# A transformer block on one core: the exact-table GELU of nine chunks becomes a tanh formula with its steps on GpSimd, and background matmuls may run as four column tiles

## The chip, the cores and the metric

The kernel runs on one core of a Trainium2 chip. A core has five engines, each with its own queue of instructions that it takes in order: TensorE (PE, matmuls; weight loads are listed apart as PEld), VectorE (DVE), ScalarE (ACT), GpSimd (POOL) and SyncE (SP, which here issues the DMAs). They meet through semaphores. The metric is the device time of one execution in microseconds; the time before is the median of three runs. In the profile a line number such as L1023 is a line of the kernel's file. Many operations are recorded through one helper and share its line (L426 in the kernel before, L435 in the changed one); those are told apart by the tiles that they write and read.

## The reference

```python
def _A_ref(x, wqkv, wo):                       # B, S, D = 1, 2048, 640; H = 32 heads of 20
    qkv = (x @ wqkv).reshape(B, S, 3, H, Dh) ...
    scores = jnp.einsum("bhqd,bhkd->bhqk", q, k) * (Dh ** -0.5)
    p = _softmax(scores, axis=-1)
    o = jnp.einsum("bhqk,bhkd->bhqd", p, v)
    return o ... @ wo

def _B_ref(x, w_gate, w_up, w_down):           # Df = 1728
    g = jnp.einsum("bsd,df->bsf", x, w_gate)
    u = jnp.einsum("bsd,df->bsf", x, w_up)
    h = _gelu(g) * u                           # jax.nn.gelu(approximate=True)
    return jnp.einsum("bsf,fd->bsd", h, w_down)

x = A_x
h = x + _A_ref(_layernorm(x), A_wqkv, A_wo)
h2 = h + _B_ref(_layernorm(h), B_w_gate, B_w_up, B_w_down)
```

All inputs and the output are bf16.

## The kernel before

**A planner sets every order.** The code does not issue instructions as it runs. It records operations (`Sched.op`) with an engine, an assumed length, a priority, the keys they read and write, and the PSUM banks they take and release. `Sched.schedule` then plays them through a model in Python and fixes each engine's order; `Sched.emit` writes that order out with the semaphore waits that the keys ask for. An engine on the chip keeps this order, so an instruction whose input is late holds back all that stands behind it on its engine. The planner knows the engines' lengths and semaphore delays; it has no notion of two engines that share a path to on-chip memory.

**Attention.** Scores are made as tiles of 128 keys x 512 (head and query pairs laid side by side): 2048 tiles, four heads to a *quad* of tiles. PE's score matmuls (L1023) use row tiles of 32 rows, up to four at once. A *unit* is three or two tiles in PSUM banks 0 to 2 or 3 and 4. ACT takes the exponential of a unit in one instruction of 1536 or 1024 columns and writes `pts` or `pts2` (in `rege`). The value matmuls (L426, out of `pts`, `rege` or others and `v_all`) use column tiles of 32 columns, four at once, and add up in bank 6. ACT can't do all exponentials in the time wanted, so some quads (78 of 512, by slot in `D_QUADS`; `D_LEAD` and `D_QUADS` also set when they start) are made on VectorE with integer tricks: each of their four tiles is evicted from PSUM by L967, then the quad takes three passes of 2048 columns that read and write SBUF alone (`d_exp`: a mask, a product, a mask). Their spare buffers are pieces of regions that are free at that time, such as old query blocks of `qt_all`.

**The MLP in the background.** The queries are cut into ten chunks (six of 256 rows, four of 128). While the attention of later chunks runs, `post` works on the chunk before: output projection, residual, layernorm (`ln_rsqrt`, whose dozen tiny steps run on POOL, and a normalise on DVE), a DMA transpose, then for blocks of up to 512 gate columns: gate matmuls (`mms`, L1227), GELU, up matmuls, product, and `down` (L1345). These matmuls use the whole array (mode `full`). PE pays some time when neighbouring matmuls change the tiling (modes `row`, `col`, `full`), and the planner charges `MODE_SWITCH` for it. `chain` makes the other background matmuls (L716: projections of queries, keys and values, and `wo`).

**GELU before.** In chunks 0 to 6 VectorE copies the gate block from PSUM, ACT applies its GELU table to up to 2048 columns at once, and VectorE multiplies by the up block. The GELU table is not the exponential's, so ACT loads a table ahead of it and another behind it; `MERGE = (0, 2, 5)` puts two chunks into one such block. In chunks 7 and 8 (`TANH`) GELU is worked out with the tanh, which needs no other table than the exponential's: three DVE steps (square, multiply-add, product) in `qt_all`, the tanh on ACT, then on DVE a step with the up block and a last product. The last chunk (`tail`) uses the GELU table after the last exponential, and is the same in both kernels.

**Zero matmuls.** Where the planner finds PE too little used over 3.4 us it adds column-tiled matmuls of zeros into bank 6 (`self.pad`, four of 512 columns a set) or a warm matmul, so that PE's clock stays up. `PAD_MIN` and `WARM_MIN` are the shares of use below which it does.

Of the kernel before, what the change touches and what calls it, by code (L numbers as in the profile page):

```python
# [7 lines left out]
ALU = mybir.AluOpType  # L8
AX = mybir.AxisListType
FP32 = mybir.dt.float32  # L10
BF16 = mybir.dt.bfloat16
# [7 lines left out]
WARM_WIN, WARM_MIN = 3.4, 0.53  # L19
PAD_WIN, PAD_MIN = 3.4, 0.46  # L20
QK_LEAD = 0.55
PE_AGE = 0.5
# [20 lines left out]
class Op:  # L43
    __slots__ = ("i", "eng", "fns", "dur", "lat", "prio", "deps", "succ", "nd", "ready",
                 "acq", "rel", "sem", "tag", "mode", "start", "fin", "pos", "know", "util")


class Sched:
# [15 lines left out]
    def op(self, eng, fns, dur, prio, reads=(), writes=(), acq=(), rel=(), after=(), sem=None, lat=None, mode=None, util=0.0):  # L64
# [6 lines left out]
        o.mode = mode  # L71
        o.tag = writes[0] if writes else None
# [24 lines left out]
    def schedule(self):  # L97
# [20 lines left out]
        live = begun = False  # L118
        due = None
        total = len(ops)  # L120
        while done < total:
# [6 lines left out]
            for e in ENGINES:  # L128
# [9 lines left out]
                while ready[e]:  # L138
# [8 lines left out]
                    if e == "pe" and due is not None and o.prio[0] > 0 and t < due < t + o.dur + (MODE_SWITCH[e] if mode[e] not in (None, o.mode) else 0):  # L147
                        skipped.append((p, i))
                        if len(skipped) >= 60:
                            break  # L150
                        continue
                    for bk in o.acq:
                        for b in bk.allowed:
                            if owner[b] is None and free_at[b] <= t + 1e-9 and b not in got and b not in kept:
                                got.append(b)
                                break
# [10 lines left out]
                    if chosen is None:  # L167
                        chosen, banks = o, got
                        if e != "pe" or p[0] < 1 or o.mode == mode[e] or t - o.ready > PE_AGE:
                            break  # L170
# [15 lines left out]
                if chosen is None:  # L186
                    if e == "pe" and self.warm is not None:
# [5 lines left out]
                        if sum(x for _, x in recent) < WARM_MIN * WARM_WIN and (free7 or live or free6):  # L193
# [3 lines left out]
                            o.acq, o.rel, o.succ, o.dur = [], [], [], 0.215  # L197
# [15 lines left out]
                t0 = t  # L213
                if o.i in self.heads:
                    self.spare = self.spares[o.tag[1]]
                    js, nk = self.heads[o.i]
# [144 lines left out]
FOUR = (28, 29)  # L361
PERM_C = 2
# [13 lines left out]
MERGE = (0, 2, 5)  # L376
TANH = (7, 8)
# [9 lines left out]
D_Q2 = 26  # L387
D_LAG = 2
D_QUADS = (0, 2, 3, 2, 2, 3, 2, 2, 3, 3, 3, 3, 3, 3, 2, 3, 2, 3, 4, 3, 2, 3, 3, 3, 2, 2, 2, 2, 2, 2, 2, 2, 0)
D_FIRST, D_PART = 2, 0.8  # L390
D_LEAD = ((0, 0, 0, 0, 0, 0, 0, 0), (0, 10, 12, 12, 12, 12, 12, 12, 12, 12, 12, 16, 16, 8, 8, 8, 12, 12, 12, 12, 12, 12, 12, 12, 8))
# [13 lines left out]
def bass_sequential_preLN__mha_block__glu_gated_geglu__prompt_kernel(  # L405
# [12 lines left out]
    with ExitStack() as es:  # L418
# [55 lines left out]
        def carver(reg, size):  # L474
            off = [0]

            def carve(n):
# [40 lines left out]
                 **{"q%d" % k: [qr[k][:, 0:2048], qr[k][:, 2048:4096]] for k in range(3)}}  # L518
# [193 lines left out]

        def chain(bk, key, n, steps, reads, prio, acq=True, after=()):
            cold = 0.1 if prio == P_PRO and not any(("xnT", tt) in reads for tt in range(4, NT)) else 0.0
            for k, (l, r) in enumerate(steps):
                yield op("pe", lambda eng, l=l, r=r, k=k: eng.matmul(  # L716
                    bank(bk, n), l, r, start=(k == 0), stop=(k == len(steps) - 1)),
                    c_mm(n) + cold, prio, mode="full", util=n / 2400.0, reads=reads, writes=[key], acq=[bk] if (k == 0 and acq) else [],
                    after=after if k == 0 else ())
# [204 lines left out]
        t_last = {}  # L924
# [6 lines left out]

        def q_free(k, lo, hi):
            return sum((tuple(last_qk[c]) for c, (q0, nq) in enumerate(QR) if c and q0 // 512 == k and lo <= q0 % 512 < hi), ())
# [4 lines left out]
        def d_regions(tile, u):  # L938
# [4 lines left out]
            return ("i",) * (tile[0] == 7) + ("k", "x", "w") + ("q0",) * (us >= 8) + ("q1",) * (us >= 16) + ("q2",) * (us >= D_Q2)  # L943

        def d_free(region):
# [4 lines left out]
            return q_done(int(region[1])) + tuple(t_last.get(4, ()) if region == "q2" else ())  # L950
# [11 lines left out]
        def d_exp(b, tile, prio, u, aft):  # L962
# [11 lines left out]
            d(I("tensor_tensor", y.bitcast(BF16), v.bitcast(BF16), y.bitcast(BF16), ALU.mult), 1.06, vk + yk, yk)  # L974
# [177 lines left out]
        gated, tanhs = [], []  # L1152
        t_last.clear()

        def post(c, first_banks, banks, tail):
# [50 lines left out]
            for tt in range(tb, tb + nt):  # L1206
# [5 lines left out]
                else:  # L1212
                    dma_transposes(o_nat[:, tt, :], [("on", g, tt) for g in range(NG)], hnT[:, :, tt * 128:(tt + 1) * 128], ("hnT", tt),
                                   after=first)
            p = P_LATE if c == len(CHUNKS) - 2 else P_BG
# [5 lines left out]
            def mms(k, w, wkey, after):  # L1221
                bk, key = Bank(*banks), ("bk", sc_id())
                for fi in range(min(fn_, NF - k * fn_)):
                    f = k * fn_ + fi
                    for a in range(NA):
# [3 lines left out]
                            start=(a == 0), stop=(a == NA - 1)),  # L1229
                           c_mm(nq), p, mode="full", util=nq / 2400.0, reads=hk + [(wkey, a)], writes=[key], acq=[bk] if st else [],  # L1230
                           after=after if st else ())
# [23 lines left out]
            elif c in TANH:  # L1255
                kq = q0 // 512
# [193 lines left out]
```

## Time and profile before

| what | value |
|---|---|
| median of 3 runs | 882.65 us (882.62 to 882.92) |
| the profiled execution | 882.6 us, its span 880.9 us |
| busy: PE, DVE, ACT, POOL | 844.7, 645.9, 852.1, 62.7 us |
| mean granted PE clock | 0.998 |
| first exponential starts, last one ends | 30.0 and 857.1 us |
| instructions: PE matmuls, DVE, ACT, POOL | 13370, 1117, 791, 194 |

A *group* row reads: line, engine, operation, out <- in, partitions x elements (or for PE rows*columns of the weights), count | busy us, mean ns of one | idle us just before them and what ended it. A *timeline* row reads: start us, length us, engine, line, operation, out <- in, size, count; neighbours of one kind are merged. Lengths of neighbours overlap on one engine, since one starts while the one before still writes. A row of the table of *stretches* gives, for from:to, the length and then busy us (count) of PE, weight loads, DVE, ACT and POOL, the granted clock, the DMA share and GB/s. A row of the *waits* reads: who waited <- for whom: us in total, times, longest.

### The profile page before, as it was taken

To read this page: it belongs to the slowest core of one execution; us is meant where nothing else is said; L and a number is where in the kernel's file an instruction comes from. 1 tells how busy PE (TensorE), PEld (TensorE's weight loads), DVE (VectorE), ACT (ScalarE), POOL (GpSimd) and SP (SyncE) were. 2 spreads that over 40 slices of the span, in tenths; PEclk is the share of its full clock that TensorE was granted. 3 is DMA by queue.
4 is the path that set the end of the run, shared out by engine and by line. 5 is a ranking of instruction groups with operands and counts; after the bars stand their busy time and mean duration, and the time that the engine had idled before them with its cause. 6 is when DMAs were issued, how large, how long until landed. Compare 5 with 4: busy or idle time off the path is not lost.

```text
span 880.9 us, 29309 instructions
## 1 busy us (share of the span) xinstructions
PE 844.7 (96%) x13370; PEld 430.9 (49%) x13370; DVE 645.9 (73%) x1117; ACT 852.1 (97%) x791; POOL 62.7 (7%) x194
## 2 busy tenths in 40 slices
PE   4999999999999999999999999999999999999998
PEld 2432322234344445444444454444565666666677
DVE  7748877776898876877778976787776574666874
ACT  7999999999999999999999999999999999999991
POOL 6600000000201000000010000010010020100200
PEclk9999999999999999999999999999999999999999
DMA  8211111442440000000100001001020100010000
GB/s 268 80 29 39 32 51 53 129 108 80 124 119 17 3 2 1 10 24 17 39 13 13 3 1 25 24 17 31 3 31 5 40 11 3 11 40 18 12 3 24
DMA packets 38763, 34.18 MB, mean 39 GB/s; under 512 B 18260, under 2 KB 36800, under 8 KB 38640
## 3 DMA queue, kind: packets, MB, share of 16 engines
q1 hardware_dynamic: 38640, 32.32, 13.4%
q8 instruction: 105, 1.72, 0.8%
q14 instruction: 18, 0.15, 0.0%
HBM read 20.12 MB, written 8.09 MB: 32 GB/s over the span
## 4 chain that ended last, share of the span: by engine, by line
ACT 67%; PE 27%; DVE 3%; POOL 2%; issue 1%; POOLq 0%
ACT pts L426 43%; ACT rege L426 23%; PE ps L1023 7%; PE ps L426 5%; PE ps L1227 5%; PE ps L716 4%; PE ps L1345 3%; ACT L426 1%; PE ps L658 1%; PE ps L1128 1%; DVE qt_all L967 1%; PE ps L821 1%; DVE qt_all L426 0%; POOL nw L426 0%; DVE stats L426 0%
## 5 line engine op out<-in xcount | busy, mean ns | idle before, releaser
L426 ACT ACTIVATE pts<-ps 128x1536 bf16<-128x1536 f32 (+1 forms) x472 | 547.1, 1293 | 2.7 <-PE ps L426 1.5
L1023 PE MATMUL ps<-qt_all,kt_all 32*128 32x256 bf16 (+2 forms) x4736 | 317.7, 257 | 13.4 <-DVE qt_all L967 3.5
L426 ACT ACTIVATE rege<-ps 128x1536 bf16<-128x1536 f32 (+1 forms) x234 | 281.3, 1292 | 1.1 <-PE ps L1023 1.0
L1023 PEld LDWEIGHTS ps<-qt_all,kt_all 32*128 32x128 bf16 x4736 | 121.6, 92 | 195.5 <-ACT pts L426 63.6
L967 DVE TENSOR_SCALAR qt_all<-ps 128x512 int16<-128x512 f32 x204 | 139.2, 687 | 62.7 <-PE ps L1023 61.9
L1227 PE MATMUL ps<-rege,regw 128*128 128x256 bf16 (+1 forms) x1400 | 166.3, 255 | 3.9 <-ACT rege L426 1.8
L1227 PEld LDWEIGHTS ps<-rege,regw 128*128 128x128 bf16 x1400 | 104.6, 98 | 53.1 <-issue 25.7
L426 PE MATMUL ps<-pts,v_all 128*21 128x256 bf16 (+2 forms) x2694 | 121.6, 259 | 0.0
L426 PE MATMUL ps<-rege,v_all 128*21 128x256 bf16 (+2 forms) x1698 | 99.6, 267 | 0.3 <-DVE rege L426 0.3
L716 PE MATMUL ps<-regw 128*128 128x512 bf16 (+1 forms) x350 | 84.3, 349 | 1.3 <-DVE rs L426 1.0
L1345 PE MATMUL ps<-regw,rege 128*128 128x320 bf16 x448 | 83.4, 302 | 0.6 <-DVE rege L1349 0.5
L426 PEld LDWEIGHTS ps<-pts,v_all 128*21 128x21 bf16 x2694 | 58.3, 91 | 27.4 <-issue 20.9
L426 PEld LDWEIGHTS ps<-rege,v_all 128*21 128x21 bf16 x1698 | 42.1, 91 | 23.8 <-issue 14.9
L967 DVE TENSOR_SCALAR rege<-ps 128x512 int16<-128x512 f32 x64 | 43.3, 686 | 12.8 <-PE ps L1023 12.3
L1345 PEld LDWEIGHTS ps<-regw,rege 128*128 128x128 bf16 x448 | 36.8, 98 | 29.7 <-issue 13.2
L1314 DVE TENSOR_TENSOR rege<-rege,ps 128x512 bf16<-128x512 bf16 (+1 forms) x46 | 31.3, 679 | 25.1 <-PE ps L1227 25.1
L716 PEld LDWEIGHTS ps<-regw 128*128 128x128 bf16 x350 | 27.9, 98 | 40.2 <-issue 24.2
L426 PE MATMUL ps<-kt_all,zer 128*32 128x512 bf16 x512 | 45.1, 385 | 0.2 <-DVE osb L426 0.2
L426 POOL CAST mv<-mv 128x4 bf16<-128x4 f32 (+2 forms) x13 | 4.5, 344 | 559.2 <-DVE mv L426 557.7
L426 DVE TENSOR_SCALAR qt_all<-qt_all 128x2048 int16<-128x2048 int16 (+2 forms) x65 | 40.6, 629 | 0.3
L1300 DVE CAST rege<-ps 128x512 bf16<-128x512 f32 (+1 forms) x46 | 31.2, 679 | 9.2 <-PE ps L1227 9.2
L426 DVE COPY osb<-ps 128x512 f32<-128x512 f32 (+2 forms) x33 | 22.2, 672 | 18.2 <-PE ps L426 18.1
(137 smaller groups left out, 705.4 us busy)
## 6 DMA issues: line engine op xcount, KB each, us to landing
q_rows<-regw SPq DMA_DIRECT2D x20, 128.0 KB, 1.7
out_dram<-rege SPq DMA_DIRECT2D x16, 160.0 KB, 2.3
regw<-in_A_wqkv_dram SPq DMA_DIRECT2D x3, 800.0 KB, 10.7
rege<-in_A_x_dram SPq DMA_DIRECT2D x7, 320.0 KB, 3.5
regw<-in_B_w_gate_dram SPq DMA_DIRECT2D x5, 432.0 KB, 3.6
regw<-in_B_w_up_dram SPq DMA_DIRECT2D x5, 432.0 KB, 3.3
rege<-in_A_x_dram SPq DMA_DIRECT2D x3, 640.0 KB, 6.4
kt_all<-k_rows SPq DMA_DIRECT2D x12, 160.0 KB
```

The lines of the kernel that those rows point to most:

```text
L426: return lambda eng: getattr(eng, method)(*args, **kwargs)
L658: op("pe", lambda eng, a=a: eng.transpose(bank16(bk, D)[:, 128 * a:128 * a + 128], src[:, a * 128:(a + 1) * 128], ident[:]), 0.055, prio, ...
L716: yield op("pe", lambda eng, l=l, r=r, k=k: eng.matmul(bank(bk, n), l, r, start=(k == 0), stop=(k == len(steps) - 1)), c_mm(n) + cold, pri ...
L821: w_readers.append(op("pe", lambda eng, k=k, t=t: eng.matmul(bank(bk)[0:32, :], sel[:, t, :], aq[t], start=(k == 0), stop=(k == len(ts) - 1)),
L967: d_ops.append(op("dve", lambda eng: eng.tensor_scalar(v[:, 512 * h:512 * h + 512], bank(b), EXP_MUL, 0.0, ALU.mult, ALU.max), c_dve(512), ...
L1023: return lambda eng: eng.matmul(out()[:, kk * nq:(kk + 1) * nq], kt_all[32 * j:32 * j + 32, g, kt * 128:(kt + 1) * 128], qt_all[32 * j:32 ...
L1128: op("pe", lambda eng, tt=tt, o=128 * (tt % nt * len(gs) + tt // nt): eng.transpose(bank(b2)[:, o:o + 128], osb[:, tt * 128:(tt + 1) * 128 ...
L1227: op("pe", lambda eng, a=a, f=f, fi=fi: eng.matmul(bank(bk)[:, fi * nq:(fi + 1) * nq], w[:, a, F0[f]:F0[f] + 128], hnT[:, a, 128 * tb:128 ...
L1300: cp.append(op("dve", lambda eng, bg=bg, fv=fv, w=w: eng.tensor_copy(fv, bank(bg, w)), c_dve(w), p, reads=[kg], writes=hkeys(k), rel=[bg], ...
L1314: hdone.append(op("dve", lambda eng, bu=bu, fv=fv, w=w: eng.tensor_tensor(fv, fv, bank(bu, w), ALU.mult), c_dve(w), p, reads=[ku] + hkeys( ...
L1345: op("pe", lambda eng, f=f, o=o, hf=hf, bk=bk: eng.matmul(bank(bk, 320), ha_f[:, o:o + 128], wd[:, f, hf * 320:(hf + 1) * 320], start=(f = ...
```

## The change

- **GELU**: `TANH` and `T_POOL` now list chunks 0 to 8 and `MERGE` is empty. All nine chunks use the tanh formula. The square, the multiply-add, the product ahead of the tanh and the last product run on POOL instead of DVE. The working buffer is the first 2048 columns of query block 0, so that block lends VectorE's quads one buffer instead of two, and the MLP part of chunks that come earlier is held until slot 7 (`held`).
- **Column tiles**: gate, up, down and `chain` matmuls carry a second form of four matmuls of 32 columns each (`four`). The planner takes it when PE is in column mode at that point.
- **Zero matmuls**: both shares lowered.
- **VectorE's quads**: 81 instead of 78, other starts; the product of 2048 columns is two of 1024 (`D_SPLIT`).
- **Bank 4** is closed to background work in units whose pattern or whose follower's pattern doesn't leave it free (`shut`).

```diff
-WARM_WIN, WARM_MIN = 3.4, 0.53
-PAD_WIN, PAD_MIN = 3.4, 0.46
+WARM_WIN, WARM_MIN = 3.4, 0.45
+PAD_WIN, PAD_MIN = 3.4, 0.38
...
+                if o.four and mode[e] == "col":
+                    o.fns, o.mode = o.four, "col"
+                    o.dur += 0.012
...
-MERGE = (0, 2, 5)
-TANH = (7, 8)
+MERGE = ()
+T_POOL = (0, 1, 2, 3, 4, 5, 6, 7, 8)
+TANH = (0, 1, 2, 3, 4, 5, 6, 7, 8)
...
+D_SPLIT = 2
-D_QUADS = (0, 2, 3, 2, 2, 3, 2, 2, 3, 3, 3, 3, 3, 3, 2, 3, 2, 3, 4, 3, 2, 3, 3, 3, 2, 2, 2, 2, 2, 2, 2, 2, 0)
+D_QUADS = (0, 3, 1, 2, 3, 2, 3, 3, 2, 3, 3, 1, 2, 3, 3, 3, 2, 3, 4, 2, 2, 4, 3, 4, 3, 2, 2, 2, 4, 3, 2, 2, 0)
...
+        def four(bk, lo, hi, l, r, start, stop):
+            return [lambda eng, j=j: eng.matmul(PS[32 * j:32 * j + 32, 512 * bk.b + lo:512 * bk.b + hi], l[:, 32 * j:32 * j + 32], r, start=start, stop=stop,
+                                                tile_position=(0, 32 * j), skip_group_check=True) for j in range(4)]
...
-            d(I("tensor_tensor", y.bitcast(BF16), v.bitcast(BF16), y.bitcast(BF16), ALU.mult), 1.06, vk + yk, yk)
+            for m in range(0, 4, 4 // D_SPLIT):
+                z = slice(512 * m, 512 * (m + 4 // D_SPLIT))
+                w = yk[m:m + 4 // D_SPLIT]
+                d(I("tensor_tensor", y[:, z].bitcast(BF16), v[:, z].bitcast(BF16), y[:, z].bitcast(BF16), ALU.mult), 1.06 / D_SPLIT, vk + w, w)
...
-                        d = lambda fn, n, r, ww, aft=(): op("dve", fn, 0.066 + n * w / 1024, p, reads=r, writes=ww, after=aft)
+                        d = lambda fn, n, r, ww, aft=(): op("dve", fn, 0.066 + n * w / 1024, p, reads=r, writes=ww, after=aft) if c not in T_POOL else \
+                            op(POOL, fn, 0.1 + (0.0022 if n > 0.3 else 0.0014) * w, p, reads=r, writes=ww, after=aft)
...
-                        hdone.append(op("dve", I("tensor_tensor", wide(fv), wide(fv), z, ALU.mult), 0.066 + 0.53 * w / 1024, p,
-                                        reads=tk + hkeys(k), writes=hkeys(k)))
-                t_last[c] = hdone[-4:]
+                        hdone.append(op("dve" if c not in T_POOL else POOL, I("tensor_tensor", fv, fv, z, ALU.mult),
+                                        0.066 + 0.53 * w / 1024 if c not in T_POOL else 0.1 + 0.0022 * w, p,
+                                        reads=tk + hkeys(k), writes=hkeys(k)))
...
-                post(c - 1, ALLB if tail else BGF[c + 1], ALLB if tail else BGC[c + 1], tail)
+                held.append(post(c - 1, ALLB if tail else BGF[c + 1], ALLB if tail else BGC[c + 1], tail))
+                next(held[-1])
+                while held and s_ >= 7:
+                    list(held.pop(0))
```

Counted over the whole program, before -> after: table loads on ACT 12 -> 4; GELUs on `rege` of 1536 to 2048 columns 13 -> 0; tanhs on `qt_all` of 512 columns 6 -> 51 and of 256 columns 2 -> 3; exponentials of 1536 columns 325 -> 325, of 1024 380 -> 374, of 512 1 -> 1; POOL steps of 512 or 256 columns 0 -> 216; column-tiled zero matmuls 512 -> 292; background matmuls as column tiles 0 -> 1796 (449 sets of four); neighbours on PE with different tilings 1685 -> 1526; masks of 2048 columns on DVE 156 -> 162, products 78 of 2048 columns -> 162 of 1024.

ACT before, at the GELU block of chunks 0 and 1 (`rege<-rege` is GELU, `<-ps` exponentials):

```order
L426 ACTIVATE rege<-ps 128x1536
L426 ACTIVATE rege<-ps 128x1024
L426 ACTIVATE pts<-ps 128x1536
L426 ACT_TABLE_LOAD
L426 ACTIVATE rege<-rege 128x2048
L426 ACTIVATE rege<-rege 128x1536
L426 ACTIVATE rege<-rege 128x2048
L426 ACTIVATE rege<-rege 128x1536
L426 ACT_TABLE_LOAD
```

ACT after, at the first blocks of chunk 0 (`qt_all<-qt_all` is a tanh):

```order
L435 ACTIVATE rege<-ps 128x1536
L435 ACTIVATE qt_all<-qt_all 128x512
L435 ACTIVATE rege<-ps 128x1024
L435 ACTIVATE pts<-ps 128x1536
L435 ACTIVATE pts<-ps 128x1024
L435 ACTIVATE pts<-ps 128x1536
L435 ACTIVATE pts<-ps 128x1024
L435 ACTIVATE qt_all<-qt_all 128x512
L435 ACTIVATE rege<-ps 128x1536
```

The unbroken GELU block between two table loads became single tanhs among the exponentials.

POOL after, in chunk 0: three steps of a block ahead of its tanh (`qt_all`), then last products (`rege<-rege,qt_all`):

```order
L435 TENSOR_TENSOR qt_all<-rege 128x512
L435 TENSOR_SCALAR qt_all<-qt_all 128x512
L435 TENSOR_TENSOR qt_all<-rege 128x512
L435 TENSOR_TENSOR qt_all<-qt_all,rege 128x512
L435 TENSOR_SCALAR qt_all<-qt_all 128x512
L435 TENSOR_TENSOR qt_all<-qt_all,rege 128x512
L435 TENSOR_TENSOR rege<-rege,qt_all 128x512 x4
```

DVE after, a piece from the middle of that work: L976 evicts score tiles, L1284 gate blocks; the rows of L435 with 2048 and 1024 columns are the passes of VectorE's quads.

```order
L976 TENSOR_SCALAR rege<-ps 128x512
L435 TENSOR_SCALAR qt_all<-qt_all 128x2048
L1284 TENSOR_SCALAR rege<-ps 128x512
L976 TENSOR_SCALAR rege<-ps 128x512 x2
L435 COPY osb<-ps 128x512
L976 TENSOR_SCALAR rege<-ps 128x512
L1284 TENSOR_SCALAR rege<-ps 128x512
L435 TENSOR_SCALAR dvx<-rege 128x2048
L976 TENSOR_SCALAR dwx<-ps 128x512 x2
L435 TENSOR_TENSOR dvx<-rege,dvx 128x1024 x2
```

POOL had no such steps before; they now run at the same time as these passes.

PE before, in the middle of the MLP work (L1023 scores in row tiles, L426 values in column tiles, L1227 gate or up):

```order
L1227 MATMUL ps<-rege,regw 128x256 x5
L426 MATMUL ps<-qt_all,v_all 21x256 x8
L1023 MATMUL ps<-qt_all,kt_all 128x256 x8
L426 MATMUL ps<-qt_all,v_all 21x256 x8
L426 MATMUL ps<-pts,v_all 21x256 x10
```

PE after, in such a stretch (L1035 scores, L435 values, L1239 gate or up as one matmul, L723 as four column tiles):

```order
L1035 MATMUL ps<-qt_all,kt_all 128x256 x12
L435 MATMUL ps<-pts,v_all 21x256 x8
L435 MATMUL ps<-rege,v_all 21x256 x8
L723 MATMUL ps<-rege,regw 32x256 x20
L1035 MATMUL ps<-qt_all,kt_all 128x256 x6
L1239 MATMUL ps<-rege,regw 128x256 x5
L1035 MATMUL ps<-qt_all,kt_all 128x256 x4
```

Where gate or up matmuls follow values, they now keep the column tiling; behind scores they are whole as before.

65 lines of the change are left out of this document (32 added, 33 removed).

## The prediction

> **What bounds the kernel now.** I read the page first, then ScalarE's (ACT's) waits between the start-up and the end, then its groups with the shapes kept apart.
>
> ```profile
> span 880.9 us, 29309 instructions
> ...
> PE 844.7 (96%) x13370; PEld 430.9 (49%) x13370; DVE 645.9 (73%) x1117; ACT 852.1 (97%) x791; POOL 62.7 (7%) x194
> ...
> ACT 67%; PE 27%; DVE 3%; POOL 2%; issue 1%; POOLq 0%
> ```
>
> The table of stretches gives the stage from the first softmax exponential to the last:
>
> ```profile
> 30.00:857.00 827.00, 806.24 (x12956) 402.13 (x12956) 612.34 (x1027) 823.03 (x736) 45.40 (x145) 1.00 0.13 33
> 739.00:742.50 3.50, 3.50 (x19) 2.51 (x18) 0.69 (x1) 3.48 (x3) 0.00 (x0) 0.51 0.00 0
> ```
>
> The columns are TensorE (PE), weight loads, VectorE (DVE), ACT, GpSimd (POOL), granted clock. Of 827.0 us ACT is busy 823.0. Its waits after the start-up:
>
> ```profile
> ACT pts L426 <- PE ps L426: 1.5, 1, 1.5
> ACT rege L426 <- PE ps L1023: 1.0, 2, 0.8
> ACT pts L426 <- PE ps L1023: 0.8, 3, 0.3
> ```
>
> Only 3.3 us. PE's 96% is a modelled figure over matmuls that overlap, while ACT hardly ever waits for it. So ACT sets the end: what leaves ACT is time won, and what makes it wait is time lost. The 30 us ahead and the 24 us behind keep their code.
>
> **ACT's own work.** Lengths in the groups overlap from one instruction to the next, so I take prices from starts in the timeline.
>
> ```profile
> 321.02 1.21 ACT L426 ACTIVATE pts<-ps 128x1024 bf16<-128x1024 f32 x1
> 321.93 2.56 ACT L426 ACTIVATE rege<-ps 128x1536 bf16<-128x1536 f32 x2
> 324.16 1.67 ACT L426 ACTIVATE pts<-ps 128x1536 bf16<-128x1536 f32 x1
> 325.85 1.28 ACT L426 ACT_TABLE_LOAD   x1
> 327.15 6.46 ACT L426 ACTIVATE rege<-rege 128x2048 bf16<-128x2048 bf16 x4
> 333.62 1.28 ACT L426 ACT_TABLE_LOAD   x1
> 334.92 2.37 ACT L426 ACTIVATE pts<-ps 128x1024 bf16<-128x1024 f32 x2
> ...
> 840.89 0.70 ACT L426 ACTIVATE qt_all<-qt_all 128x512 f16<-128x512 f16 x1
> 841.41 3.36 ACT L426 ACTIVATE pts<-ps 128x1024 bf16<-128x1024 f32 x3
> ```
>
> An exponential of 1024 columns takes 321.93 - 321.02 = 0.91 us. One tanh of 512 takes 841.41 - 840.89 = 0.52. The GELU block of chunks 0 and 1 keeps ACT from the softmax for 334.92 - 325.85 = 9.07 us, 2.6 of them in two table loads. All blocks together:
>
> ```profile
> L426 ACT ACT_TABLE_LOAD x12 | 15.4, 1283 | 1.0 <-PEq L1435 0.8
> L426 ACT ACTIVATE rege<-rege 128x2048 bf16<-128x2048 bf16 x6 | 11.4, 1905 | 0.0
> L426 ACT ACTIVATE rege<-rege 128x1536 bf16<-128x1536 bf16 x6 | 8.8, 1467 | 0.0
> ...
> L426 ACT ACTIVATE rege<-rege 128x1792 bf16<-128x1792 bf16 x1 | 1.7, 1678 | 0.0
> ```
>
> The order says that 8 of the 12 loads go, and all 13 GELUs: 8 x 1.283 + 11.4 + 8.8 + 1.7 = 32.2 us out. It adds 45 tanhs of 512 columns and one of 256: 45 x 0.52 + 0.3 = 23.7 us in. The three more quads for VectorE take 12 tiles from ACT, which the order shows as six exponentials of 1024 fewer: 6 x 0.91 = 5.5 us out. Net 14.0 us. The profiled execution is 882.6 us, within 0.1 of the runs' median of 882.65, so the change alone would give 882.6 - 14.0 = 868.6.
>
> **What GpSimd then does to VectorE.** All 54 blocks of gate columns bring POOL four steps each, 216 in all: a square, a multiply-add and a product ahead of the tanh, and the last product behind it. Until now POOL is nearly idle in this stage, and the trace has no two-input step of that size on it. The nearest rows, from the start-up and from later:
>
> ```profile
> 15.21 0.87 POOL L426 TENSOR_SCALAR rege<-rege,mu,rs 128x640 bf16<-128x640 bf16 x1 [0.79 <-DVE mv L426]
> 15.40 0.86 DVE L426 TENSOR_SCALAR rege<-rege,mu,rs 128x640 bf16<-128x640 bf16 x1
> L426 DVE TENSOR_SCALAR o_nat<-rege,mu,rs 128x640 bf16<-128x640 bf16 x16 | 6.8, 442 | 0.2
> ...
> 232.92 1.22 DVE L426 TENSOR_TENSOR rege<-dwx,rege 128x2048 bf16<-128x2048 bf16 x1
> 233.13 1.05 POOL L426 CAST mv<-mv 128x4 bf16<-128x4 f32 x1 [7.64 <-DVE mv L426]
> L426 POOL CAST mv<-mv x13: 186/190/1054, 8.3 to 819.8; 128x4 bf16<-128x4 f32 x6, 128x8 bf16<-128x8 f32 x4, 128x2 bf16<-128x2 f32 x3
> ```
>
> They shut each other out. The DVE normalise that started 0.19 us into POOL's took 0.86 instead of 0.44 us and ended just behind it. In the other direction a POOL cast of median 0.19 us took 1.05 and ended with VectorE's product. Price of a POOL step of 512 columns: with one input 0.87 x 512 / 640, about 0.7; with two inputs at least that and at most twice that, as if they were read one after the other, so 0.7 to 1.4. I take the middle, 1.05, since neither end has a nearer row. A block is then 0.7 + 3 x 1.05 = 3.85 us, 53 blocks (three narrow ones count half) about 203 us, with ends 147 and 260. By the order the first tanh has 224 exponentials ahead of it and the last nearly all, so this lies in some 570 us: POOL holds the access 36% of that time (26 to 46%).
>
> VectorE's passes that read and write SBUF alone are the ones that meet it:
>
> ```profile
> L426 DVE TENSOR_SCALAR qt_all<-qt_all 128x2048 int16<-128x2048 int16 x57 | 38.8, 681 | 0.3
> L426 DVE TENSOR_TENSOR dvx<-qt_all,dvx 128x2048 bf16<-128x2048 bf16 x18 | 22.0, 1220 | 0.2
> ```
>
> Between the first gate copy and the last gated product the order has 121 such masks, 121 half products and 13 normalises among 766 rows, 255 in all. A pass that comes while POOL holds waits on average half of POOL's mean step of 0.96 us: 255 x 0.36 x 0.48 = 44 us of delay on VectorE (26% of a 0.7 step: 23; 46% of a 1.23 step: 72). VectorE is idle for 215 us of the stage and can take that as a sum, but what stands behind a late pass is a score tile's eviction or a product that PE waits for in its order. How much reaches ACT is the unknown term, between none and all 44 us. The nearest row is the score matmuls' own idle time:
>
> ```profile
> L1023 PE MATMUL ps<-qt_all,kt_all 32*128 32x256 bf16 (+2 forms) x4736 | 317.7, 257 | 13.4 <-DVE qt_all L967 3.5
> ```
>
> Of 13.4 us that PE waited here, ACT's rows show 1.8 behind it, about one seventh. VectorE's idle time would make the share smaller and its chains of four passes larger, so I take that row's: one in seven, 6 us.
>
> The Trainium skill has the same rule (SBUF — State Buffer, section Who interferes with whom): such VectorE instructions and GpSimd take turns, and the later one is fully blocked. By that rule the trace agrees, 0.86 against 0.44 us. The Trainium skill (GPSIMD Engine Reference, section 3.1) also puts a two-input step at about 2.6 cycles an element, as an estimate 1.1 us for 512 elements plus dispatch; at 1.3 a block would be 4.6 us, and the same steps would give 62 us of delay, 9 on ACT, and a time of 877.6.
>
> **The rest of the change** costs nothing on ACT; the cover of each is ACT's own queue.
>
> ```profile
> L426 PE MATMUL ps<-kt_all,zer 128*32 128x512 bf16 x512 | 45.1, 385 | 0.2 <-DVE osb L426 0.2
> L426 PEld LDWEIGHTS ps<-pts,v_all 128*21 128x21 bf16 x2694 | 58.3, 91 | 27.4 <-issue 20.9
> 791.45:792.00 0.56, 0.56 (x38) 0.45 (x32) 0.41 (x1) 0.56 (x2) 0.00 (x0) 1.00 0.00 0
> L967 DVE TENSOR_SCALAR qt_all<-ps 128x512 int16<-128x512 f32 x204 | 139.2, 687 | 62.7 <-PE ps L1023 61.9
> ```
>
> Four column tiles: the value products already run so. The stretch from 791.45 to 792.00 holds nothing else, 32 of them with a weight load each (the second count): 0.07 us for a set of four, less than one load's 91 ns, so sets and loads overlap. So the 449 converted matmuls cost PE no more than one whole matmul each, and the order has 1526 changes of tiling where it had 1685. 220 fewer zero matmuls take 220 / 512 x 45.1 = 19 us off PE's busy time. Both ease an engine that costs ACT 3.3 us at most: 0 to 3.3 us of gain, I take 0. If the zeros' absence lets the clock drop, see the rivals. A half product takes at least 0.61 us (half of 1.22) and at most a mask's 0.68: up to 81 x 2 x 0.07 = 11 us more on DVE. Three quads add 3 x (4 x 0.69 + 2 x 0.68 + 1.22) = 16 us, the tanh steps of chunks 7 and 8 leave it. VectorE's 215 us of idle time cover this with 188 to spare; without that cover it would be 27 us on the path. The layernorm's small POOL steps of the next chunk now queue among the GELU steps, up to a step's 1.05 us behind each; who waits for them are a DVE normalise, a transposing DMA on SP and background matmuls, none of which ACT reads. The last gated product of chunk 8 is a POOL step now: about 1 us ahead of matmuls that the tail runs anyway.
>
> Sum: 882.6 - 32.2 + 23.7 - 5.5 + 6 = 874.6.
>
> **The rivals.** (1) *Slower: the port.* The late passes reach ACT nearly in full, because PE takes its instructions in order and a late eviction holds back the next score matmuls. It decides once more than 14.0 / 44 = 32% of VectorE's delay reaches ACT; at 60% it is 26 us: 882.6 - 14.0 + 26 = 895. For it: an exponential of 0.91 or 1.3 us (324.16 - 321.93 less 0.91) is all that PE has to refill a bank. Against it: VectorE's 26% idle time.
> (2) *The collisions are hidden.* None of the 44 us reaches ACT: 868.6. For it: POOL's small steps of today cost nothing that ACT's waits show.
> (3) *POOL paces the tanh.* ACT takes the tanhs in order, often three to five exponentials apart. A block's three steps of 0.7 + 2 x 1.05 = 2.8 us, with two waits of up to 1.2 for VectorE's products, exceed the 3.3 us of three exponentials. At 0.25 us for each of 54 tanhs on top of the sum: 874.6 + 13.5 = 888. It also ends slower.
> (4) *The clock.* The second row of the table of stretches shows 0.51 granted where PE had little to do in a GELU block. That block goes, but less padding could bring such stretches elsewhere. One of 3.5 us loses 1.7 us of PE's work; four would cost 7: 881.6.
>
> **How the numbers follow.** Tell-apart is 0.2%, 1.8 us. Forecast (870 to 880): 0.50. Rival 2 (865 to 870, since the 3.3 us of waits can go as well): 0.13. Rival 1: 0.23. Rival 3: 0.09. Rival 4: 0.05. Faster is the forecast and rival 2, less the forecast's upper edge: 0.62. Same is that edge, rival 4 and a little of rival 3: 0.09. Slower is rival 1 and the rest of rival 3: 0.29. The predicted time is the likeliest case's 874.6, with 870 to 880 as its own range. The whole range is 865 to 893: it leaves out the worse half of rival 1 and a little below.
>
> **What the changed profile would show.** Right: four table loads, no ACT gap of 6 to 9 us, ACT busy for about 809 us of its stage, POOL near 265 us busy, and DVE masks with a mean above 0.69 us. A stage in which ACT waits under 15 us bears the one in seven out. Wrong: ACT rows that wait for POOL (rival 3), score matmuls that wait 40 us for L976 (rival 1), or PEclk under 1.00 in several stretches (rival 4). A two-input POOL step over 1.4 us would break the price on which the collisions rest.

## The result: slower, and the profile after

The changed kernel takes 902.76 us (median of 4 runs, 900.25 to 910.03) against 882.70 for the kernel before on the same chip: a ratio of 1.0241, interval 1.0216 to 1.0266. It is 28 us over the forecast of 874.6 and above its range of 865 to 893. The profiled execution is 902.66 us.

The page after, the three lines that answer to those of before:

```profile
span 901.1 us, 32084 instructions
...
PE 828.6 (92%) x14532; PEld 428.9 (48%) x14556; DVE 693.7 (77%) x1187; ACT 844.5 (94%) x810; POOL 296.8 (33%) x410
...
PE 39%; ACT 27%; DVE 27%; POOL 4%; issue 1%; DMA 0%; SPq 0%; POOLq 0%
```

ACT's busy time fell by 7.6 us, and the span rose by 20. The chain that ended last was 67% ACT and 3% DVE; now it is 27% each, with PE first. The chain no longer runs along ACT's queue but hops between PE and VectorE.

The table of stretches, from the first softmax exponential to the last, and one of the half-clock places below it (columns PE, PEld, DVE, ACT, POOL, granted clock):

```profile
30.00:878.00 848.00, 791.63 (x14127) 400.51 (x14147) 659.88 (x1097) 815.97 (x757) 277.73 (x359) 0.99 0.13 32
429.50:432.90 3.40, 3.40 (x48) 1.76 (x43) 1.83 (x4) 1.28 (x2) 0.00 (x0) 0.50 0.00 0
```

ACT was without work for 827.0 - 823.0 = 4.0 us of this stage before; now for 848.0 - 816.0 = 32.0. ACT's waits (us in total, times, longest):

```profile
ACT pts L435 <- PE ps L1035: 17.2, 27, 2.1
ACT rege L435 <- PE ps L1035: 7.5, 12, 1.3
...
ACT qt_all L435 <- POOL qt_all L435: 3.7, 7, 1.3
```

PE's waits in the same view, which lie behind those of ACT:

```profile
PE ps L435 <- DVE qt_all L435: 9.0, 13, 1.8
PE ps L435 <- DVE dvx L435: 4.7, 7, 1.0
PE ps L435 <- DVE rege L435: 4.0, 7, 1.1
...
PE ps L1035 <- DVE dwx L976: 2.8, 8, 0.7
...
PE ps L1035 <- DVE rege L976: 2.6, 12, 0.3
...
PE ps L435 <- DVE dwx L435: 1.8, 4, 0.5
...
PE ps L1035 <- DVE qt_all L976: 1.4, 5, 0.4
```

ACT waits 24.7 us for score matmuls (1.8 before). PE waits 19.5 us (9.0 + 4.7 + 4.0 + 1.8) ahead of the value products of the quads, whose inputs VectorE's masks and half products write, and 6.8 us (2.8 + 2.6 + 1.4) ahead of score matmuls for the evictions on L976. In the kernel before, the longest row of the first kind was this:

```profile
PE ps L426 <- DVE qt_all L426: 0.7, 2, 0.4
```

The passes that meet POOL are the ones that grew (groups with their shapes):

```profile
L435 POOL TENSOR_TENSOR qt_all<-qt_all,rege 128x512 f16<-128x512 f16 x51 | 66.0, 1294 | 4.2
...
L435 DVE TENSOR_TENSOR dvx<-rege,dvx 128x1024 bf16<-128x1024 bf16 x50 | 41.9, 858 | 0.3
L435 DVE TENSOR_SCALAR rege<-rege 128x2048 int16<-128x2048 int16 x53 | 41.5, 786 | 0.6
...
L435 POOL TENSOR_SCALAR qt_all<-qt_all 128x512 f16<-128x512 f16 x51 | 37.3, 731 | 4.4
...
L435 DVE TENSOR_TENSOR rege<-rege 128x1024 bf16<-128x1024 bf16 x28 | 18.3, 684 | 0.1
```

The last row is the half product of the slots ahead of the first GELU step: 0.684 us undisturbed, as against 0.858 for those of the first `dvx` row, of which 44 of 50 start behind the first step. One place in the timeline shows the whole path:

```profile
424.71 1.47 POOL L435 TENSOR_TENSOR qt_all<-qt_all,rege 128x512 f16<-128x512 f16 x1
425.21 1.52 DVE L435 TENSOR_TENSOR dvx<-rege,dvx 128x1024 bf16<-128x1024 bf16 x1
...
427.37 0.47 DVE L1151 TENSOR_TENSOR o_nat<-ps,rc 128x320 bf16<-128x320 f32 x1
427.59 1.15 POOL L435 TENSOR_TENSOR rege<-rege,qt_all 128x512 bf16<-128x512 bf16 x1 [1.41 <-DVE qt_all L1296]
427.76 1.52 DVE L435 TENSOR_TENSOR dvx<-rege,dvx 128x1024 bf16<-128x1024 bf16 x1
427.90 0.29 PE L723 MATMUL ps<-rege,regw 128*32 128x256 bf16 x4 [0.99 <-DVE o_nat L1151]
...
429.34 0.48 PE L435 MATMUL ps<-dvx,v_all 128*21 128x256 bf16 x8 [0.82 <-DVE dvx L435]
```

A half product that starts 0.50 us into a POOL step takes 1.52 instead of 0.68 us; a second one does the same 2.5 us on. Behind it on VectorE the eviction on L1151 is late, so a background matmul that PE has in its queue waits 0.99 us, then the value product 0.82 us; the score matmuls stand behind both in that queue, and ACT runs dry from about 429.6. At 429.5 the granted clock halves for 3.4 us.

### The profile page after: what moved, and what is told of

Read it like the earlier page. It is cut to its first block, busy times and chain, and to the rows that moved or that the text cites. A ratio compares the mean times of both kernels' runs of the same rounds, so it can differ in the third digit from the quotient of the medians.

```text
span 901.1 us, 32084 instructions
## 1 busy us (share of the span) xinstructions
PE 828.6 (92%) x14532; PEld 428.9 (48%) x14556; DVE 693.7 (77%) x1187; ACT 844.5 (94%) x810; POOL 296.8 (33%) x410
## 4 chain that ended last, share of the span: by engine, by line
PE 39%; ACT 27%; DVE 27%; POOL 4%; issue 1%; DMA 0%; SPq 0%; POOLq 0%
ACT pts L435 18%; PE ps L1035 12%; ACT rege L435 9%; DVE qt_all L435 8%; PE ps L435 8%; PE ps L1239 7%; PE ps L1354 5%; DVE dvx L435 4%; PE ps L729 3%; PE ps L723 3%; DVE qt_all L976 3%; DVE rege L976 3%; DVE dwx L976 3%; POOL qt_all L435 2%; DVE qt_all L1296 2%; DVE rege L1284 1%
## 5 line engine op out<-in xcount | busy, mean ns | idle before, releaser
L435 ACT ACTIVATE pts<-ps 128x1536 bf16<-128x1536 f32 (+1 forms) x467 | 545.2, 1284 | 20.3 <-PE ps L1035 17.2
L1035 PE MATMUL ps<-qt_all,kt_all 32*128 32x256 bf16 (+2 forms) x4736 | 320.5, 258 | 22.5 <-ACT pts L435 3.0
L435 ACT ACTIVATE rege<-ps 128x1536 bf16<-128x1536 f32 (+2 forms) x233 | 280.3, 1283 | 7.8 <-PE ps L1035 7.5
L1035 PEld LDWEIGHTS ps<-qt_all,kt_all 32*128 32x128 bf16 x4736 | 119.6, 92 | 211.1 <-ACT pts L435 64.9
L1239 PE MATMUL ps<-rege,regw 128*128 128x256 bf16 (+1 forms) x1121 | 131.4, 253 | 4.5 <-DVE rege L1284 1.4
L976 DVE TENSOR_SCALAR rege<-ps 128x512 int16<-128x512 f32 x156 | 106.1, 685 | 30.5 <-PE ps L1035 29.9
L435 POOL TENSOR_TENSOR qt_all<-rege 128x512 f16<-128x512 bf16 (+1 forms) x54 | 61.2, 1133 | 184.7 <-DVE rege L1284 181.9
L435 PE MATMUL ps<-pts,v_all 128*21 128x256 bf16 (+2 forms) x2646 | 120.8, 260 | 0.0
L435 PE MATMUL ps<-rege,v_all 128*21 128x256 bf16 (+2 forms) x1710 | 100.7, 268 | 4.2 <-DVE rege L435 4.0
L1239 PEld LDWEIGHTS ps<-rege,regw 128*128 128x128 bf16 x1121 | 81.3, 98 | 42.6 <-issue 21.8
L435 POOL TENSOR_TENSOR rege<-rege,qt_all 128x512 bf16<-128x512 bf16 (+1 forms) x54 | 65.6, 1215 | 72.4 <-DVE qt_all L1296 70.2
L976 DVE TENSOR_SCALAR dwx<-ps 128x512 int16<-128x512 f32 x92 | 62.6, 685 | 22.7 <-PE ps L1035 22.7
L435 PEld LDWEIGHTS ps<-pts,v_all 128*21 128x21 bf16 x2646 | 58.0, 91 | 26.7 <-issue 21.5
L435 POOL TENSOR_TENSOR qt_all<-qt_all,rege 128x512 f16<-128x512 f16 (+1 forms) x54 | 68.5, 1268 | 4.4
L976 DVE TENSOR_SCALAR qt_all<-ps 128x512 int16<-128x512 f32 x76 | 51.7, 685 | 19.0 <-PE ps L1035 18.9
L435 POOL MEMSET regw<- 128x128 bf16 (+1 forms) x2 | 0.8, 416 | 175.0 <-DMA bounds<-regw 175.0
L435 PEld LDWEIGHTS ps<-rege,v_all 128*21 128x21 bf16 x1710 | 43.3, 91 | 29.7 <-issue 13.7
L1296 DVE SCALAR_TENSOR_TENSOR qt_all<-qt_all,ps 128x512 bf16<-128x512 f16 (+1 forms) x54 | 35.8, 665 | 19.1 <-PE ps L1239 17.6
L1284 DVE TENSOR_SCALAR rege<-ps 128x512 bf16<-128x512 f32 (+1 forms) x54 | 36.1, 669 | 15.3 <-PE ps L1239 11.6
L723 PE MATMUL ps<-rege,regw 128*32 128x256 bf16 (+1 forms) x1116 | 44.5, 265 | 2.2 <-DVE o_nat L1151 1.0
```

The costliest lines, as they stand in the source:

```text
L435: return lambda eng: getattr(eng, method)(*args, **kwargs)
L723: return [lambda eng, j=j: eng.matmul(PS[32 * j:32 * j + 32, 512 * bk.b + lo:512 * bk.b + hi], l[:, 32 * j:32 * j + 32], r, start=start, s ...
L976: d_ops.append(op("dve", lambda eng: eng.tensor_scalar(v[:, 512 * h:512 * h + 512], bank(b), EXP_MUL, 0.0, ALU.mult, ALU.max), c_dve(512), ...
L1035: return lambda eng: eng.matmul(out()[:, kk * nq:(kk + 1) * nq], kt_all[32 * j:32 * j + 32, g, kt * 128:(kt + 1) * 128], qt_all[32 * j:32 ...
L1239: op("pe", lambda eng, a=a, f=f, fi=fi: eng.matmul(bank(bk)[:, fi * nq:(fi + 1) * nq], w[:, a, F0[f]:F0[f] + 128], hnT[:, a, 128 * tb:128 ...
L1284: op("dve", lambda eng, bg=bg, fv=fv, w=w: eng.tensor_scalar(fv, bank(bg, w), 0.5, None, ALU.mult), c_dve(w), p, reads=[kg], writes=hkeys( ...
```

## Experiments

Fifteen kernels ran, each against the kernel before on the same chip. The table has those on VectorE's delay; the others stand in the text. A ratio is that to the kernel before; "idle" is the stretch from the first exponential to the last less ACT's busy time in it.

| run | time us | ratio (interval) | DVE busy us | ACT idle us |
|---|---|---|---|---|
| changed kernel | 902.76 | 1.0241 (1.0216-1.0266) | 693.7 | 32.0 |
| e1 short POOL steps | 864.95 | 0.9800 (0.9786-0.9815) | 655.5 | 2.3 |
| e5 each pass in two | 875.81 | 0.9921 (0.9907-0.9936) | 675.6 | 7.0 |
| e11 masks in four | 892.84 | 1.0109 (1.0089-1.0130) | 697.1 | 19.6 |
| e7 POOL in five chunks | 896.43 | 1.0172 (1.0141-1.0202) | 709.8 | 23.0 |
| e6 planner avoids | 882.02 | 0.9988 (0.9978-0.9997) | 674.7 | 6.5 |
| e15 e6 with 79 quads | 872.77 | 0.9885 (0.9870-0.9900) | 662.1 | 5.2 |
| e3 steps on VectorE | 880.88 | 0.9982 (0.9972-0.9991) | 712.6 | 7.6 |
| e8, e14 e3 with 80 quads | 870.53, 868.02 | 0.9865 (0.9850-0.9880), 0.9832 (0.9816-0.9848) | 706.6, 711.1 | 2.8, 2.7 |

**e1: the port, or the rest of the change?** "The port" is short for VectorE's passes and POOL's steps shutting each other out of on-chip memory. POOL's GELU steps keep their number and place and handle 2 columns, so the GELU values are left out.

```
-  d(I("tensor_tensor", z, f2, f2, ALU.mult), ...)
+  z2, f22 = z[:, 0:2], f2[:, 0:2]
+  d(I("tensor_tensor", z2, f22, f22, ALU.mult), ...)
...
```

> The 216 GELU steps on POOL handle 2 columns instead of 512 (the GELU values are left out, so the output is not the reference's); every engine's order and the planner's costs stay as in the changed kernel. Theory port (VectorE's passes wait for POOL's steps, PE for VectorE, ACT for PE): VectorE's masks fall from 0.785 to about 0.69 us, ACT's lost time from 48.6 to about 15 us, the time to 868 to 873. Theory clock (fewer zero matmuls let the clock halve, which starves ACT): half-clock windows stay, time 885 or more. Theory pace (ACT waits for POOL's late steps): only the 4 to 6 us of ACT's waits ahead of a tanh go, time 895 to 898. Theory column tiles (sets of four cost PE more than planned): time stays near 901.

Measured 864.95 us: 37.8 less than the changed kernel. Its page, and then its stage in the table of stretches:

```profile
PE 818.2 (95%) x14532; PEld 428.9 (50%) x14556; DVE 655.5 (76%) x1187; ACT 836.5 (97%) x810; POOL 124.2 (14%) x410
```

```profile
31.00:842.00 811.00, 781.86 (x14160) 401.01 (x14179) 622.00 (x1097) 808.71 (x758) 107.32 (x360) 1.00 0.14 34
```

Same order on every engine, VectorE 38.2 us less busy, ACT idle 2.3 us, clock 1.00. ACT's busy time in the stage is 808.7 us here and 816.0 in the changed kernel, since its instructions overlap less where gaps stand between them; the gaps and this together make the 37.0 us by which the stage is shorter. So the length of POOL's steps is the whole loss, and without it the change gains 17.7 us.

**e2, e4: zeros and column tiles, with the long POOL steps.** e2 puts the old thresholds back, e4 turns the column tiles off.

```
e2
-  WARM_WIN, WARM_MIN = 3.4, 0.45
-  PAD_WIN, PAD_MIN = 3.4, 0.38
+  WARM_WIN, WARM_MIN = 3.4, 0.53
+  PAD_WIN, PAD_MIN = 3.4, 0.46
e4
-  o.four = four
+  o.four = None
```

> The two shares for zero matmuls back to 0.53 and 0.46, all else as changed. Theory clock: granted clock 1.00, time 870 to 880. Theory port: the clock comes back to 1.00 but the time gains only what four half-clock windows cost, 4 to 8 us: 894 to 899. Theories pace and column tiles: no change beyond 3 us.

> No column tiles for background matmuls, all else as changed. Theory column tiles: 870 to 880. Theory port: 900 to 908, since PE gets about 160 more changes of tiling back, some 15 us of its time, and has less room to make up for late passes.

e2: 919.24 us (1.0416, 1.0387 to 1.0445). More zeros did not hold the clock up: over its four runs the mean granted clock was 0.983 to 0.994, as against 0.983 to 0.996 in the changed kernel, and the two profiled runs have six and four half-clock stretches in the stage. e4: 935.39 us (1.0608, 1.0576 to 1.0639). So neither part causes the loss: in this order each makes the loss smaller.

The clock is not the cause either: e1 has as few zeros and none of these stretches in its stage, and in the 3.4 us ahead of each of the changed kernel's four PE was busy for only 1.6 to 2.4 us. Its price can be estimated from the changed kernel's four runs. One less the mean clock, times the span, gives between 3.6 us (900.25 us, clock 0.996) and 15.4 us (910.03 us, clock 0.983) of PE's time lost, so some eight tenths of it seem to reach the end; for the profiled run, which lost 7.2, that is about 6 of the 37.8 us.

**e9, e10, e13: the same two parts with VectorE on time.** Their edits on top of e1 (GELU values left out).

> The run with short GpSimd steps (864.95 us; GELU values left out as there) without column tiles. With long steps they were worth 32.6 us (902.8 to 935.4). If PE's time is free as long as VectorE is on time, as the prediction held (cover: ACT's queue, 0 to 3.3 us): 864 to 868 us. If the column tiles carry part of the result by themselves, because PE binds wherever eight or nine background chains fall in a slot: 885 to 898 us.

> The run with short GpSimd steps (864.95 us; GELU values left out as there) with the old thresholds for zero matmuls, 0.53 and 0.46. With long steps they cost 16.5 us (902.8 to 919.2). If zeros only fill PE's idle time while VectorE is on time: 864 to 868 us. If they take PE time that is wanted: 875 to 882 us.

e9: 893.58 us (1.0114, 1.0095 to 1.0133), e10: 879.95 (0.9959, 0.9943 to 0.9975): 28.6 and 15.0 us lost without any collision. But in e9 one gap of ACT, the 12.3 of the row below, holds much of that, at 242 to 254 us, while PE runs zeros and waits for VectorE, as two rows of the timeline show:

```profile
ACT pts L435 <- PE ps L435: 14.2, 3, 12.3
```

```profile
247.29 1.05 PE L435 MATMUL ps<-kt_all,zer 128*32 128x512 bf16 x16
249.19 0.29 PE L435 MATMUL ps<-rege,v_all 128*21 128x256 bf16 x4 [0.85 <-DVE rege L435]
```

PE is not short of time there; the order has ACT wait for quads of VectorE. So e13 gave e9 its own numbers of quads per slot (79 in all):

> The run with short GpSimd steps and without column tiles (893.58 us; GELU values left out as there), with 79 quads instead of 81 spread in another way over the slots (D_QUADS). If PE's time is free and the 28.6 us came from an order whose numbers fit other chains: 867 to 874 us, with no ACT gap over 3 us before the tail. If the column tiles' PE time is needed by itself: 882 to 894 us.

e13: 872.28 us (0.9880, 0.9865 to 0.9895), with no such gap. Of the 28.6 us, 21.3 came from an order whose numbers fit the column tiles. The other 7.3, two quads fewer included, are what the tiles are worth between these two orders. Numbers that fit the old zeros were not tried, so for the 15.0 us the same split is open.

**e5, e11: delay without collisions.** e1 with masks and half products cut into pieces. A cut costs about 0.07 us, as a half product in two pieces and a single piece (both e5) and one uncut (e1) show:

```profile
202.67 0.76 DVE L435 TENSOR_TENSOR rege<-rege 128x512 bf16<-128x512 bf16 x2
...
205.76 0.42 DVE L435 TENSOR_TENSOR rege<-rege 128x512 bf16<-128x512 bf16 x1
...
203.34 0.69 DVE L435 TENSOR_TENSOR rege<-rege 128x1024 bf16<-128x1024 bf16 x1
```

```
-  d(I("tensor_scalar", y, v, 0x7F, 0x3F00, ...), 0.53, vk, yk)
+  d(cut(2, 2048, lambda z: I("tensor_scalar", y[:, z], v[:, z], 0x7F, 0x3F00, ...)), 0.53, vk, yk)
...
e11
-  cut(2, 2048, ...)
+  cut(4, 2048, ...)
```

> The run with short GpSimd steps (864.95 us) with every VectorE mask pass issued as two instructions over half the columns, and every half product as two: 4 more instructions in each of the 81 quads, 324 in all. By the rows of the run with the steps on VectorE (0.286 us for a mask over 512 columns, 0.685 over 2048; 0.418 us for a product over 512, 0.68 over 1024) one split adds at most 0.15 us, so VectorE gets at most 49 us more, and probably 20 to 45; the planner is not told. GELU values are left out as in the run it starts from. Theory A, the total of the delay decides: as in the changed kernel some 8 to 9 tenths of what VectorE loses reach the end, so 885 to 905 us. Theory B, unevenness decides (single passes that take 0.5 to 0.9 us more than planned, several in a row): delays of 0.1 us on each pass are taken up by VectorE's idle time, under 0.25 of the added time reaches the end, 866 to 875 us.

> As the run with evenly delayed passes (875.81 us: one split added 0.07 us by its timeline, VectorE's busy time rose by 20.1 us, the end by 10.9), with each mask in four pieces: 8 more instructions in each of the 81 quads, about 45 us more on VectorE than with whole passes, a little more than the 40 us that collisions took in the changed kernel. GELU values are left out as there. If unevenness makes a collision's delay twice as costly as an even one: half of it reaches the end again, 885 to 890 us. If the size of the delay decides and the loss grows faster than the delay (10 for 20, 38 for 40): 899 to 910 us, with ACT's gaps behind PE and half-clock windows as in the changed kernel.

e5: VectorE 20.1 us busier than e1, the end 10.9 later (54%). e11: 41.6 busier, 27.9 later (67%), with ACT's waits, and the one stretch at half clock (the column ahead of the last two):

```profile
ACT pts L435 <- PE ps L1036: 8.0, 25, 0.7
ACT rege L435 <- PE ps L1036: 7.5, 17, 1.4
```

```profile
263.80:267.10 3.30, 3.30 (x47) 1.46 (x47) 3.02 (x11) 1.99 (x2) 2.05 (x9) 0.50 0.12 42
```

Both results fall between the two expectations. Delay spread evenly, an estimated 0.07 us (one cut) to 0.21 us (three cuts) a pass, with no long POOL steps, costs more than half of itself, and the share was larger for the larger delay. Collisions cost more again: 37.8 for 38.2 us (99%). The rows hold most of the 9.9 us between this and e11: ACT's 3.7 us of waits for POOL's steps, and three more stretches at half clock, 1.7 us of PE's work each. No run took these two away, so this split is by rows alone.

**e7: fewer collisions.** `T_POOL = (0, 2, 4, 6, 8)`; the other chunks' steps run on VectorE.

> The changed kernel with the GELU steps on GpSimd for chunks 0, 2, 4, 6 and 8 only; those of 1, 3, 5 and 7 run on VectorE. Short GpSimd steps took 37.8 us off the changed kernel. If each collision costs its share of the end (linear, about six tenths of the 51 groups of steps stay on GpSimd): 865 + 0.6 x 38 = 888 us, 884 to 892. If VectorE's and PE's slack takes up the first part of the delay, so that the loss grows faster than the number of collisions: 868 to 878 us. If the loss is set by a few bad places: outside both, over 893 or unchanged.

896.43 us, which is the last case by its number; whether a few bad places set the loss was not tested. About half of the blocks (27 of the 51 full ones) brought 31.5 of the 37.8 us. The delay had not halved: VectorE's masks and half products lost 26 us to the steps here and 38 in the changed kernel, by their lengths in the two traces less those in e1. The steps that moved also took VectorE to 80% busy. So the loss is no fixed price per block; how much of it is the fuller VectorE is open.

**e12: the halved product.** `D_SPLIT = 1`.

> The changed kernel with the product of a quad in one VectorE instruction over 2048 columns instead of two over 1024 (about 1.29 us undisturbed by the rows of the halves, 0.69 and 0.60 behind it). If halving is worth nothing by itself (the delay is set by GpSimd's time on the port): 898 to 907 us. If a whole product makes an eviction behind it late by 0.6 us more each time: 908 to 925 us. If fewer, longer passes meet fewer GpSimd steps: 885 to 897 us.

906.93 us (1.0265, 1.0230 to 1.0300), which the intervals do not tell from the changed kernel. The planner's order moved too: the last exponential ends at 866.6 instead of 878.1 us, the tail (what stands behind it) is 15 us longer, and ACT's waits for POOL's steps rise from 3.7 to 15.6 us. What halving does by itself stays open.

**e6, e15: the same work in an order that knows of the port.** In the planner POOL's steps and VectorE's masks and products hold one resource:

```
+  if o.port and held > t + 0.05:
+      events.append(held)
...
+      skipped.append((p, i))
...
+      continue
...
+  if o.port:
+      o.dur += max(0.0, held - o.start)
+      held = o.start + o.dur
```

> The changed kernel with one rule more in the planner: GpSimd's GELU steps and VectorE's masks and half products hold one shared resource, and neither starts while the other holds it; another instruction of VectorE goes first instead. The work is the same, the order differs. The plan's end of the exp stage stands 3 us earlier than in the changed kernel, but seven tanhs more fall behind the last exp, so the tail is about 13 us longer. Theory B (delays that the order does not know of stall PE's queue, then ACT's): the masks come back to 0.69 to 0.72 us, ACT's gaps shrink to about those of the kernel with short GpSimd steps, and the time is 872 to 882 us, of which 13 us is the longer tail. Theory A (the lost VectorE and GpSimd time itself is what costs): the planned waits cost the same as the unplanned ones, 895 to 910 us.

e6: 882.02 us, 20.7 less than the changed kernel, with POOL as busy (293.6 us). ACT idles 6.5 us of its stage instead of 32.0:

```profile
30.00:844.00 814.00, 776.81 (x13933) 394.75 (x13951) 635.05 (x1089) 807.49 (x750) 253.38 (x335) 1.00 0.13 34
```

But chunk 8's GELU now runs into a tail of 36.7 us, in which ACT waits 12.7 us for POOL. The new order did not end the collisions, it halved them: 37 of VectorE's 324 masks and half products still take over 0.1 us longer than in e1 (64 in the changed kernel), and VectorE is still 19.2 us busier than in e1 (38.2 there). That rest is of the size of e5's 20.1 us, and so is ACT's idle time (6.5 and 7.0 us). e15 mends the tail by numbers of quads:

> The planner that keeps GpSimd's steps and VectorE's passes apart (882.02 us, of it a tail of 36.7 us behind the last exp) with 79 quads instead of 81 spread in another way (D_QUADS), so that chunk 8 is done ahead of the last exp. If only the tail kept it back: 869 to 875 us, ACT's gaps as in that run. If the remaining collisions weigh more in the new order: 878 to 890 us.

e15: 872.77 us. Its page, and its stage:

```profile
PE 819.0 (94%) x14586; PEld 428.6 (49%) x14586; DVE 662.1 (76%) x1171; ACT 841.3 (97%) x813; POOL 292.4 (34%) x410
```

```profile
30.00:848.00 818.00, 783.65 (x14200) 401.96 (x14198) 629.10 (x1082) 812.80 (x760) 273.99 (x359) 1.00 0.13 34
```

POOL is nearly as busy as in the changed kernel (292.4 against 296.8 us), and ACT idles 5.2 us. So the same steps did not have to cost what they did: an order that keeps them apart from VectorE's passes has about half of the delay, and the keeping apart costs ACT little. That a delay of the same size would be cheap if only the order knew of it is not shown.

**e3, e8, e14: no GELU steps on POOL.** `T_POOL = ()` puts the steps on VectorE.

> All nine chunks by tanh, but the steps on VectorE (54 blocks x about 1.5 us = 80 us more work there, none on POOL). Theory port: passes no longer stretched (masks 0.69 us), the planner knows of all the work; ACT's lost time 15 to 25 us, time 868 to 880. Theory clock: half-clock windows stay, 885 or more. Theory column tiles: near 900. Rival to port, VectorE simply too full: 885 to 900 with VectorE above 85% busy.

> The run with all GELU steps on VectorE (880.88 us, of which the tail behind the last exp was 35.5 us instead of 23) with 80 quads instead of 81 and spread differently over the slots (D_QUADS), so that chunk 8's steps are done ahead of the last exp; one exp of about 1 us more. If the long tail was what kept that run from 868 us: 867 to 872 us, tail 22 to 26 us. If VectorE at 81% busy is itself the bound, the tail's loss moves into the stage: 877 to 884 us.

> All GELU steps on VectorE, 80 quads in a spread of its own (the run of that kind before it: 870.53 us with a tail of 26 us). If the tail and ACT's own work are what is left: 865 to 869 us. If VectorE at 81% is the bound: 870 us again or more.

e3: 880.88 us. Its stage is short, its tail 35.2 us, as chunk 8's GELU comes too late:

```profile
30.00:844.00 814.00, 777.96 (x14008) 397.29 (x14029) 669.70 (x1286) 806.36 (x751) 42.86 (x145) 1.00 0.14 34
844.00:879.20 35.20, 30.27 (x397) 24.53 (x384) 18.80 (x52) 10.32 (x15) 0.00 (x0) 0.99 0.05 15
```

With 80 quads, spread in other ways, the tail is 26.3 us (e8, 870.53) and 23.5 (e14). e14 is the fastest kernel here that computes everything: 868.02 us, 1.7% under the kernel before, with VectorE 82% busy.

## Why the prediction was wrong, point by point

- **ACT's own work: right.** Forecast was 809 us of ACT work in the stage. e1, where nothing is late, shows 808.7, and ends 17.7 us ahead of the kernel before, where the sum had 14.0 and up to 3.3 more from ACT's old waits.
- **POOL's price: a little low.** Two-input steps took 1.16 to 1.29 us in the mean (taken: 1.05, bounds 0.7 and 1.4), one-input 0.73 (0.7); POOL's total is 297 us (265). The medians are 1.04 to 1.16 and 0.62; the means hold longer steps, such as the 1.47 us one at 424.71, which started while a VectorE mask ran. The Trainium skill (GPSIMD Engine Reference, section 3.1) gives 2.6 cycles an element, an estimate of 1.1 us for 512 elements before dispatch. The medians agree with it.
- **VectorE's delay: right in its way and nearly in size.** Forecast 44 us, measured 693.7 - 655.5 = 38.2. The rule of the Trainium skill (SBUF — State Buffer, Who interferes with whom), that the later of the two is shut out, agrees: 0.68 became 1.52 us behind a POOL step.
- **The share of it that reaches ACT: the step that failed.** "One in seven, 6 us" was 37.8 of 38.2 us. Rival 1 had the mechanism and 26 us. The one in seven was misread to start with: the 13.4 us in its row are not all waits for VectorE. In the view of PE's waits before, 4.5 of them are behind ACT itself (the larger row is below), and those behind VectorE add up to 5.6.

```profile
PE ps L1023 <- ACT pts L426: 3.4, 10, 0.5
```

By these alone the share would have been a third, 14 us and a time of some 883, still far too low. It was also a share of waits in an order made with VectorE's lengths known; probably they stood where ACT had scores in store. Delays that the order did not know of reached the end at 54% and 67% when spread evenly, and at 99% in collisions. The last figure holds ACT's waits for POOL and the clock as well.

- **VectorE's idle time as cover: also wrong.** The prediction let VectorE take the delay "as a sum", saw that a late pass holds up what stands behind it, and still held the 26% idle time against rival 1. VectorE was idle for 811.0 - 622.0 = 189 us of e1's stage; e11 put 41.6 us more on it, and 27.9 reached the end. So idle time over four times the delay covered a third of it.
- **Where PE waits: half right.** Rival 1 named the evictions on L976. They account for 6.8 us of the score matmuls' waits; the value products behind late masks and half products wait 19.5 us.
- **Column tiles and zeros at nothing: right in the sum, wrong in its ground.** The cover was said to be ACT's queue. But putting one or the other back costs 28.6 or 15.0 us in this order, and 7.3 (tiles) between two orders that each fit. The tiles are worth little as PE time, and much as what the numbers of quads were set for; for the zeros this is not shown.
- **Rivals 3 and 4** are small: ACT waits 3.7 us for POOL (13.5 forecast for the rival), and four stretches at half clock cost 6.8 us of PE's work. In e1's stage neither appears. POOL's lateness is not gone for good: in e6 ACT waits 12.7 us for it in the tail.

## What to carry to other kernels

In a kernel whose engines run an order fixed ahead, price a change by what the order doesn't know: here a delay outside the plan reached the end at half to all of its size, though VectorE had over four times as much idle time, while an order that kept the two engines apart ran the same steps with half of the delay and a fifth of ACT's idle time. A share taken from waits that an order already contained was no measure of new ones. And before a part is judged by taking it out, give the order's hand-set numbers a chance to fit: 21 of 29 us in e9, and 12 us of e3's tail, hung on such numbers.

## What the runs showed of the hardware

- More zero matmuls did not hold the clock up here. The kernel with 552 of them and PE stalls (e2) ran at a mean granted clock of 0.983 to 0.994, the changed kernel with 292 at 0.983 to 0.996, and the one with 292 and no stalls (e1) at 1.000.
- A VectorE mask or half product that started inside a POOL step of the GELU was shut out until the step ended, with two exceptions. In the changed kernel 77 of them started so, and 70 ended 0.54 to 0.55 us after the step did, whatever was left of it; two took their usual 0.68 us inside the step. The half product at 425.21 came 0.50 us into a 1.47 us step and ended 0.55 us after it.
- Cutting a 0.68 us VectorE pass in two costs about 0.07 us, though an instruction over half the columns is listed at 0.42: the two together take 0.76, so they overlap.
